# A decode block on one core: w2 taken up in six pieces instead of five, and the first wq issued from ScalarE's queue

## The chip, the core and the metric

The kernel runs on one core of a Trainium2 chip. The metric is the device time of one execution in microseconds, the median of several runs. The profile is of one execution; its span goes from the first instruction to the last, and its times count from the span's start. Engines: PE is TensorE (PEld its weight loads), DVE is VectorE, ACT is ScalarE, POOL is GpSimd, SP is SyncE, which here issues nearly all DMAs. A DMA started by SP stands in SP's queue (SPq), one started by ACT in ACT's (ACTq).

## The reference

One token for each of 4 batch rows goes through an adaptive-layernorm transformer block in float32: attention with 32 query heads on 8 key/value heads over the last 2048 positions of a cache, then a SwiGLU of width 1792, each with a gate. The six modulation vectors come from c:

```
mod = (silu(c) @ w_mod).reshape(4, 6, 1, 512)
sa, ca, ga, sb, cb, gb = mod[:, 0], ..., mod[:, 5]
h = layernorm(x) * (1 + ca) + sa
x = x + ga * attention(h, k_cache, v_cache, wq, wo)   # wq: 512 x 4096, wo: 4096 x 512
h = layernorm(x) * (1 + cb) + sb
x = x + gb * ((silu(h @ w1) * (h @ w3)) @ w2)          # w1, w3: 512 x 1792, w2: 1792 x 512
```

attention: q = h @ wq in 32 heads of 128; of k_cache and v_cache (4 x 8 x 8192 x 128) only the last 2048 positions are used, each kv head by 4 query heads; scores times 128^-0.5, softmax, times v, then @ wo.

## The kernel before, in words

With 4 tokens there is hardly any reuse: every weight and every used part of the cache is read from HBM once, 101 MB in all. The kernel is one stream of large loads on SP's queue, with all compute placed beside it. Each engine has its own program, and semaphores join them. Two SBUF buffers of 8 MB, KV[0] and KV[1], take in turn the k and v of one kv head each (8 heads, `kv_in[g]`); WP (4 MB) takes wo of two heads and wq of the next two.

**The front.** T0 lies in KV[1] and takes t0_in: c and the two parts of w_mod for ca and sa (2 MB). The upper half of WP takes t1_in: wq of the first two heads (2 MB). SP issues T0, then t1, then KV[0], then waits for `pe` >= 1 (the products bM = silu(c) @ w_mod are done with T0) before it loads KV[1]. ACT issues x (8 KB) as its first instruction. VectorE and ACT compute the statistics of x (helpers `stats` and `rroot`, L152 to L169), then, later in both programs, silu(c) (L182 to L188, tile sc). TensorE forms bM from sc, then VectorE forms h (L195), TensorE transposes it, forms the first head's q (bQ, from WP), turns it, and VectorE lays it out in Z (L206). Only then, and once KV[0] has landed, come the first scores (bS from KV and Z).

**The loop.** TensorE runs a loop over 4 pairs of heads: scores, transposed probabilities, values (bO from KV and pT), and the output projection, which gathers in bA. SP issues each load as soon as the buffer it goes to has been read; `s_done`, `o_done`, `q_done`, `a_done` count what TensorE has finished.

**The tail.** After the last head SP issues, behind one another, the rest of w_mod, w1 and part of w3, the rest of w3 in two pieces, gb's part of w_mod (`dgb`), and w2. w2 has 14 chunks of 128 rows (CHUNKS gives their order); W2_CUTS cuts them into pieces, each with its own semaphore dw[i]. hidT holds the hidden activations, transposed. On TensorE, in program order: the two feed-forward products, bM (gb for 4 tokens, four partial sums), then the first HEAD = 8 chunks into bO, 512 columns each, four partial sums at partitions 0, 32, 64, 96; then bT, which sums gb's parts and lays it out by columns (with the 0/1 matrix `same`); then the other six chunks into bX, in the laid-out form, four products of 128 columns for each chunk. VectorE copies bO to y_sb (L459), and four products with `same` add y_sb to bX. ACT copies gb to gb_sb (L448) and bT to gbJ (L465). At the end VectorE multiplies bX by gbJ (yt, L478), adds x (y, L480), and SP stores 64 KB.

Every product goes through one helper line, L266, and most transposes through L287, so in the profile they are told apart by tiles. All SP loads are at L89.

Of the kernel before, what the change touches and what calls it, by code (L numbers as in the profile page):

```python
# [10 lines left out]
B, D, HQ, G, SK, DH, W, FF = 4, 512, 32, 8, 8192, 128, 2048, 1792  # L11
P = 128
# [2 lines left out]
EPS = 1e-5  # L15
CHUNKS = [(j, c) for c in range(4) for j in range(4) if c < 2 or j < 3]
HEAD = 8
W2_CUTS = [0, 8, 10, 12, 13, 14]
PAIRS = G // 2


# [22 lines left out]
def block_kernel(nc, x_in, t0_in, t1_in, kv_in, w_in, wm_in, f1_in, f2_in, gb_in, w2_in, out):  # L44
    T, v, s, gp, S = nc.tensor, nc.vector, nc.scalar, nc.gpsimd, nc.sync

    def sems(names):
        return [nc.alloc_semaphore(n) for n in names.split()]

    def sb(name, cols, rows=P):  # L50
        return nc.alloc_sbuf_tensor(name, (rows, cols), F32).ap()

    def bank(name):
        return nc.alloc_psum_tensor(name, (P, 512), F32).ap()

    (first,) = sems("first")
    A = Queue(nc, s, "act")
    V = Queue(nc, v, "dve")
    L = Queue(nc, gp, "pool")
    dx, dt0, dt1, dkv, dk, dva, dvb, dwo, dm, df1, df2a, df2b, dgb = sems("dx dt0 dt1 dkv dk dva dvb dwo dm df1 df2a df2b dgb")  # L60
    dw = sems(" ".join(f"dw{i}" for i in range(len(W2_CUTS) - 1)))
    z_ok, q_ok, p_ok, k_ok, va_ok, vb_ok, pt_ok, o_ok, ot_ok = sems("z_ok q_ok p_ok k_ok va_ok vb_ok pt_ok o_ok ot_ok")
    s_done, q_done, qt_done, pp_done, o_done, x_done, a_done, pe, last = sems("s_done q_done qt_done pp_done o_done x_done a_done pe last")
# [3 lines left out]
    WP = sb("WP", 8192)  # L67
    T0 = KV[1][:, : 16 + 4096]
    x_sb = sb("x_sb", 512, B)
    ident, same, eps = sb("ident", P), sb("same", B), sb("eps", 1)  # L70
# [3 lines left out]
    q_sb, p_sb, o_sb, a_sb, y_sb, g_sb, u_sb, gb_sb = [sb(n, 512) for n in "q_sb p_sb o_sb a_sb y_sb g_sb u_sb gb_sb".split()]  # L74
# [7 lines left out]
    x1J, gbJ, yt, y = [sb(n, P) for n in "x1J gbJ yt y".split()]  # L82
    zero = y_sb

    bS, bQ, bT, bP, bO, bX, bA, bM = [bank(n) for n in "bS bQ bT bP bO bX bA bM".split()]


    def load(dst, src, sem):
        S.dma_start(dst, src).then_inc(sem, 16)  # L89

    load(T0, t0_in, dt0)
    s.dma_start(x_sb, x_in).then_inc(dx, 16)
    load(WP[:, 4096:], t1_in, dt1)
    load(KV[0], kv_in[0], dkv)
    S.wait_ge(pe, 1)
    load(KV[1], kv_in[1], dk)
# [26 lines left out]
    load(KV[1][:, 6144:8192], gb_in, dgb)  # L123
    for a, b, sem in zip(W2_CUTS[:-1], W2_CUTS[1:], dw):
        load(KV[1][:, 8192 + a * 512 : 8192 + b * 512], w2_in[:, a * 512 : b * 512], sem)
# [139 lines left out]
    def mm(o, lhsT, rhs, start=True, stop=True):  # L265
        return T.matmul(o, lhsT, rhs, start=start, stop=stop, skip_group_check=True)  # L266
# [46 lines left out]
    for k in range(4):  # L313
        for i in range(2):
            ins = mm(bM[32 * i : 32 * i + B, :], sc[:, k * B : (k + 1) * B], T0[:, 16 + (2 * k + i) * 512 : 16 + (2 * k + i + 1) * 512], k == 0, k == 3)
    ins.then_inc(pe, 1)
    T.wait_ge(V.sem, t_h[1])
    for k in range(4):
        ins = T.transpose(bT[:, k * B : (k + 1) * B], h[:, k * P : (k + 1) * P], ident[:B, :B])
# [51 lines left out]
    for k in range(4):  # L371
        for i in range(3):
            at = (3 * k + i) * 512
            ins = mm(bX[32 * i : 32 * i + B, :], sc[:, k * B : (k + 1) * B], KV[0][:, at : at + 512], k == 0, k == 3)
# [19 lines left out]
    for k in range(4):  # L394
        ins = T.transpose(bT[:, k * B : (k + 1) * B], h[:, k * P : (k + 1) * P], ident[:B, :B])
# [4 lines left out]
    def view(t_):  # L400
        return t_.rearrange("p (c j i) -> p c j i", c=4, j=4)
# [4 lines left out]
    for k in range(4):  # L406
        for j in range(4):
            at = 6144 + k * 2048 + j * 512
            ins = mm(bQ[32 * j : 32 * j + B, :], h2T[:, k * B : (k + 1) * B], KV[0][:, at : at + 512], k == 0, k == 3)
# [3 lines left out]
    for k in range(4):  # L413
# [5 lines left out]
        for j in range(3):  # L419
            at = k * 1536 + j * 512  # L420
            ins = mm(bA[32 * j : 32 * j + B, :], h2T[:, k * B : (k + 1) * B], KV[1][:, at : at + 512], k == 0, k == 3)
# [14 lines left out]
    for c in range(4):  # L436
        ins = T.transpose(bS[:, c * P : c * P + 96], u_sb[:96, c * P : (c + 1) * P], ident[:96, :96])
# [6 lines left out]
    for k in range(4):  # L444
        ins = mm(bM[32 * k : 32 * k + B, :], sc[:, k * B : (k + 1) * B], KV[1][:, 6144 + 512 * k : 6144 + 512 * (k + 1)])
    ins.then_inc(pe, 1)
    A.wait((pe, 10))
    t_gb = A.op(s.copy(gb_sb, bM))  # L448
    T.wait_ge(V.sem, t_hid[1])
    hw = view(hidT)  # L450
    w2 = KV[1][:, 8192 : 8192 + 14 * 512].rearrange("p (n m) -> p n m", n=14)
    T.wait_ge(dw[0], 16)
    for n in range(HEAD):
        j, c = CHUNKS[n]
        i = n % 4
        ins = mm(bO[32 * i : 32 * i + B, :], hw[:, c, j, :], w2[:, n, :], n < 4, n >= HEAD - 4)
    ins.then_inc(pe, 1)
    V.wait((pe, 11))
    t_y = V.op(v.tensor_copy(y_sb, bO))  # L459
    T.wait_ge(A.sem, t_gb[1])  # L460
    for j in range(4):
        ins = mm(bT[32 * j : 32 * j + B, :P], same, gb_sb[:, j * P : (j + 1) * P])
    ins.then_inc(pe, 1)
    A.wait((pe, 12))
    t_gb = A.op(s.copy(gbJ, bT[:, :P]))  # L465
    for i in range(1, len(W2_CUTS) - 1):
        T.wait_ge(dw[i], 16)
        for n in range(W2_CUTS[i], W2_CUTS[i + 1]):
            jj, c = CHUNKS[n]
            for j in range(4):  # L470
                ins = mm(bX[32 * j : 32 * j + B, :P], hw[:, c, jj, :], w2[:, n, j * P : (j + 1) * P], n == HEAD, n == 13)
        if i == 1:
            T.wait_ge(V.sem, t_y[1])
            for j in range(4):
                mm(bX[32 * j : 32 * j + B, :P], same, y_sb[:, j * P : (j + 1) * P], False, False)
# [56 lines left out]
```

## Time and profile before

| | before |
|---|---|
| runs, us | 243.27, 244.55, 245.59; median 244.55 |
| the profiled execution, us | 245.33 in all, its span 244.0 |
| mean granted TensorE clock | 0.81 |
| busy: PE / DVE / ACT | 138.5 (57%) / 38.6 (16%) / 25.2 (10%) us |
| DMA | 101.34 MB, mean 415 GB/s over the span |
| HBM read / written | 101.20 MB / 0.07 MB |

A row of the timeline has start and duration in us, engine, line, operation, output tile, input tiles, and in brackets how long the engine was idle before and what ended that. float32 products are recorded as two instructions each, so x16 stands for 8 products. A row on DMA issues has the destination, the source, the issuing queue, how often, the size in KB of one, and the time from issue to landing. A row of stretches has its limits, its length, the busy time of PE, PEld, DVE, ACT and POOL with the number of instructions, the granted clock of TensorE (1.00 is full), the mean busy share of the DMA engines, and GB/s.

### The profile page before, as it was taken

How to read it: one execution, taken by the hardware profiler on the slowest of the kernel's cores; microseconds unless marked ns; L12 is line 12 of the kernel's file. 1: busy time of each engine (PE TensorE's matmuls, PEld its weight loads, DVE VectorE, ACT ScalarE, POOL GpSimd, SP SyncE). 2: the span in 40 equal slices, each digit the busy share in tenths (PEclk: the TensorE clock that was granted, in tenths of full speed). 3: DMA queues.
4: the chain of work that ended last, by engine and by line, in shares of the span. 5: the costliest groups of instructions: out<-in, count | busy, mean ns of one | idle time of the engine just before them, and what ended most of it. 6: DMA issues, size and time to landing. Idle time of an engine off the chain costs nothing. (4 is left out here: it accounts for less than half of the span.)

```text
span 244.0 us, 2237 instructions
## 1 busy us (share of the span) xinstructions
PE 138.5 (57%) x940; PEld 39.2 (16%) x940; DVE 38.6 (16%) x126; ACT 25.2 (10%) x54; POOL 1.7 (1%) x14
## 2 busy tenths in 40 slices
PE   3451047826771477278615763696057758728756
PEld 0010001301220112012101220121012221202203
DVE  6020002202200022022000320220004022150202
ACT  4010001101010021001100210002002111060100
POOL 2000000000000000000000000000000000000000
PEclk9995557988798589767975996779659988997967
DMA  7998999989898989898989898989899999999980
GB/s 255 430 521 346 505 430 430 451 387 500 381 494 365 505 365 496 355 505 365 494 365 494 365 494 355 505 365 494 379 432 446 418 416 434 445 397 426 434 352 16
DMA packets 3901, 101.34 MB, mean 415 GB/s; under 512 B 436, under 2 KB 564, under 8 KB 1080
## 3 DMA queue, kind: packets, MB, share of 16 engines
q1 hardware_dynamic: 3888, 101.26, 96.9%
q8 instruction: 3, 0.05, 0.1%
q10 hardware_dynamic: 8, 0.01, 0.0%
q14 instruction: 2, 0.02, 0.0%
HBM read 101.20 MB, written 0.07 MB: 415 GB/s over the span
## 5 line engine op out<-in xcount | busy, mean ns | idle before, releaser
L266 PE MATMUL bS<-KV,Z 128*16 128x512 f32 x256 | 44.4, 857 | 53.1 <-PEq L269 53.1
L266 PE MATMUL bO<-KV,pT 128*16 128x512 f32 x256 | 31.0, 626 | 0.5
L266 PEld LDWEIGHTS bS<-KV,Z 128*16 128x16 f32 x256 | 9.5, 126 | 82.3 <-issue 82.3
L222 DVE TENSOR_REDUCE MX<-bS 128x1 f32<-128x512 f32 x8 | 5.5, 692 | 95.9 <-PE bS L266 95.9
L230 ACT ACTIVATE p_sb<-bS,NB 128x512 f32<-128x512 f32 x8 | 5.5, 687 | 116.6 <-DVE NB L228 116.6
L287 PE MATMUL bP<-ident,p_sb 128*128 128x128 f32 x32 | 6.2, 329 | 16.6 <-PEq L269 16.6
L266 PE MATMUL bA<-WP,oT 128*4 128x512 f32 x64 | 11.7, 811 | 3.1 <-PEq L269 3.1
L266 PEld LDWEIGHTS bO<-KV,pT 128*16 128x16 f32 x256 | 8.0, 105 | 23.2 <-issue 23.2
L251 ACT ACTIVATE o_sb<-bO,LB 128x512 f32<-128x512 f32 x8 | 5.5, 687 | 47.3 <-PE bO L266 47.3
L287 PE MATMUL bX<-ident,o_sb 128*128 128x128 f32 x32 | 5.0, 280 | 7.2 <-PEq L269 7.2
L266 PE MATMUL bM<-KV,sc 128*4 128x512 f32 x24 | 6.0, 713 | 4.8 <-DVE sc L188 4.8
L266 PE MATMUL bQ<-WP,hT 128*4 128x512 f32 x64 | 8.3, 592 | 0.6 <-DVE hT L197 0.6
L254 DVE TENSOR_REDUCE oT<-bX 128x16 f32<-128x64 f32 x8 | 1.8, 225 | 41.4 <-PE bX L287 41.4
L287 PEld LDWEIGHTS bP<-ident,p_sb 128*128 128x128 f32 x32 | 4.1, 164 | 24.0 <-issue 24.0
L287 PE MATMUL bT<-ident,q_sb 128*128 128x128 f32 x32 | 5.3, 292 | 3.2 <-PEq L269 3.2
L201 ACT ACTIVATE q_sb<-bQ 128x512 f32<-128x512 f32 x8 | 4.7, 593 | 12.5 <-PE bQ L266 12.5
L287 PEld LDWEIGHTS bX<-ident,o_sb 128*128 128x128 f32 x32 | 3.4, 142 | 14.3 <-issue 14.3
L235 DVE COPY pT<-bP 128x256 f32<-128x256 f32 x8 | 3.4, 425 | 14.2 <-PE bP L287 14.2
L266 PE MATMUL bQ<-KV,h2T 128*4 128x512 f32 x32 | 5.1, 799 | 0.3 <-DVE h2T L398 0.3
L266 PE MATMUL bO<-KV,hidT 128*4 128x512 f32 x16 | 3.6, 1047 | 2.7 <-DMA KV<-w_in 2.7
L287 PEld LDWEIGHTS bT<-ident,q_sb 128*128 128x128 f32 x32 | 3.5, 144 | 7.1 <-issue 6.8
L266 PE MATMUL bX<-KV,sc 128*4 128x512 f32 x24 | 4.1, 592 | 0.0
(100 smaller groups left out, 65.4 us busy)
## 6 DMA issues: line engine op xcount, KB each, us to landing
WP<-w_in SPq DMA_DIRECT2D x3, 4096.0 KB, 21.9
KV<-kv_in SPq DMA_DIRECT2D x1, 4096.0 KB, 24.6
KV<-f_in SPq DMA_DIRECT2D x1, 4096.0 KB, 28.1
KV<-kv_in SPq DMA_DIRECT2D x1, 3072.0 KB, 31.4
KV<-wm_in SPq DMA_DIRECT2D x1, 3072.0 KB, 18.7
KV<-f_in SPq DMA_DIRECT2D x2, 1536.0 KB, 19.1
KV<-t_in SPq DMA_DIRECT2D x1, 2056.0 KB, 7.7
WP<-t_in SPq DMA_DIRECT2D x1, 2048.0 KB, 12.2
```

The source lines that it names most:

```text
L201: A.op(s.mul(q_sb, bQ, DH**-0.5), q_ok)
L222: t = V.op(v.reduce_max(MX[:, 0:1], bS, axis=AX.X))
L230: A.op(s.activation(p_sb, bS, AF.Exp, bias=NB[:, 0:1], accum_out=SM[:, 0:1]), p_ok)
L235: v.tensor_copy(pT.rearrange("p (t b c r) -> p c b t r", t=NT, b=B, c=4), bP.rearrange("p (c b i) -> p c b i", c=4, b=B)[:, :, :, :16].rea ...
L251: A.op(s.mul(o_sb, bO, LB[:, 0:1]), o_ok)
L254: V.op(v.tensor_reduce(oT.rearrange("p (r b) -> p r b", r=R), diag, axis=AX.X, op=ALU.add), ot_ok)
L266: return T.matmul(o, lhsT, rhs, start=start, stop=stop, skip_group_check=True)
L287: ins = T.transpose(dst[:, c * P : (c + 1) * P], src[:, c * P : (c + 1) * P], ident)
```

## The change

Two places change. First, W2_CUTS: the 8-chunk first piece of w2 becomes two pieces of 4 chunks, each with its own semaphore. TensorE waits for the first, forms the first four bO products, then bT, then waits for the second, forms the other four, and goes on with bX as before. The signals of bT and bO swap their places in the count `pe`, and the copies gbJ and y_sb wait accordingly. Second, t1 (the first wq) is no longer issued by SP behind T0, but by ACT, as its first instruction; x follows it in ACT's queue, and KV[0] follows T0 at once in SP's.

```diff
-W2_CUTS = [0, 8, 10, 12, 13, 14]
+W2_CUTS = [0, 4, 8, 10, 12, 13, 14]
...
     load(T0, t0_in, dt0)
+    s.dma_start(WP[:, 4096:], t1_in).then_inc(dt1, 16)
     s.dma_start(x_sb, x_in).then_inc(dx, 16)
-    load(WP[:, 4096:], t1_in, dt1)
     load(KV[0], kv_in[0], dkv)
     S.wait_ge(pe, 1)
     load(KV[1], kv_in[1], dk)
...
-    T.wait_ge(dw[0], 16)
-    for n in range(HEAD):
-        j, c = CHUNKS[n]
-        i = n % 4
-        ins = mm(bO[32 * i : 32 * i + B, :], hw[:, c, j, :], w2[:, n, :], n < 4, n >= HEAD - 4)
-    ins.then_inc(pe, 1)
-    V.wait((pe, 11))
-    t_y = V.op(v.tensor_copy(y_sb, bO))
-    T.wait_ge(A.sem, t_gb[1])
-    for j in range(4):
-        ins = mm(bT[32 * j : 32 * j + B, :P], same, gb_sb[:, j * P : (j + 1) * P])
-    ins.then_inc(pe, 1)
-    A.wait((pe, 12))
-    t_gb = A.op(s.copy(gbJ, bT[:, :P]))
-    for i in range(1, len(W2_CUTS) - 1):
+    for i in range(len(W2_CUTS) - 1):
         T.wait_ge(dw[i], 16)
         for n in range(W2_CUTS[i], W2_CUTS[i + 1]):
             jj, c = CHUNKS[n]
+            if n < HEAD:
+                ins = mm(bO[32 * (n % 4) : 32 * (n % 4) + B, :], hw[:, c, jj, :], w2[:, n, :], n < 4, n >= HEAD - 4)
+                continue
             for j in range(4):
                 ins = mm(bX[32 * j : 32 * j + B, :P], hw[:, c, jj, :], w2[:, n, j * P : (j + 1) * P], n == HEAD, n == 13)
+        if i == 0:
+            T.wait_ge(A.sem, t_gb[1])
+            for j in range(4):
+                ins = mm(bT[32 * j : 32 * j + B, :P], same, gb_sb[:, j * P : (j + 1) * P])
+            ins.then_inc(pe, 1)
+            A.wait((pe, 11))
+            t_gb = A.op(s.copy(gbJ, bT[:, :P]))
         if i == 1:
+            ins.then_inc(pe, 1)
+            V.wait((pe, 12))
+            t_y = V.op(v.tensor_copy(y_sb, bO))
+        if i == 2:
             T.wait_ge(V.sem, t_y[1])
             for j in range(4):
                 mm(bX[32 * j : 32 * j + B, :P], same, y_sb[:, j * P : (j + 1) * P], False, False)
```

On TensorE, at the end of the program, the order changes as follows (- before, + now; KV holds w2, hidT the hidden activations, dw0, dw1, ... are the pieces' semaphores, act and dve those of ScalarE and VectorE):

```order
 L266 MATMUL bM<-KV,sc 4x512 x3
 L266 MATMUL bO<-KV,hidT 4x512 [waits dw0,dve]
-L266 MATMUL bO<-KV,hidT 4x512 x7
+L266 MATMUL bO<-KV,hidT 4x512 x3
 L266 MATMUL bT<-gb_sb,same 4x128 [waits act]
 L266 MATMUL bT<-gb_sb,same 4x128 x3
-L266 MATMUL bX<-KV,hidT 4x128 [waits dw1]
+L266 MATMUL bO<-KV,hidT 4x512 [waits dw1]
+L266 MATMUL bO<-KV,hidT 4x512 x3
+L266 MATMUL bX<-KV,hidT 4x128 [waits dw2]
 L266 MATMUL bX<-KV,hidT 4x128 x7
 L266 MATMUL bX<-y_sb,same 4x128 [waits dve]
```

The second four bO products have moved behind bT and wait for a semaphore of their own.

On ScalarE, at the start of the program (WP<-t_in is the first wq, 2 MB):

```order
-L92 DMA x_sb<-x_in 4x512 [waits barrier_Pool_Activation_PE_DVE_SP_release]
+L92 DMA WP<-t_in 128x4096 [waits barrier_Pool_Activation_PE_DVE_SP_release]
+L93 DMA x_sb<-x_in 4x512
 L171 ACT_TABLE_LOAD
 L154 ACTIVATE sq,st<-x_sb,st 4x512 [waits dve]
```

x now stands second in ScalarE's queue, behind the 2 MB of wq; SyncE's row for the same transfer is gone, and the first kv block follows T0 there.

## The prediction

> **What bounds the kernel now.** I read the page first: its slices, its queues and its chain.
>
> ```profile
> GB/s 255 430 521 346 505 430 430 451 387 500 381 494 365 505 365 496 355 505 365 494 365 494 365 494 355 505 365 494 379 432 446 418 416 434 445 397 426 434 352 16
> q1 hardware_dynamic: 3888, 101.26, 96.9%
> ```
>
> One slice is 6.1 us. The load runs at some 430 GB/s from the second slice to the last but one, and SyncE's queue alone (q1) holds the 16 DMA engines for 96.9% of the span. So the middle of the kernel is a stream of 101 MB at one rate, and a change can win only ahead of the stream, behind it, or by a hole in it. The chain of waits, in order of time, shows what stands behind it (start, us):
>
> ```profile
> 208.07 27.21 DMA KV<-w_in
> ...
> 235.41 3.59 PE bO L266 x16
> 239.01 0.43 PE bT L266 x8
> 239.43 2.32 PE bX L266 x56
> 241.78 0.30 DVE yt L478
> ...
> ```
>
> The chain hangs on the first, 8-chunk piece of w2, which lands at 235.3; after it comes 6.5 us of TensorE work in a row. Then I asked for the landings of the later pieces, by the window of their issue (issue start in the first column, then the time to landing):
>
> ```profile
> 207.58 0.44 SPq L89 DMA_DIRECT2D KV<-gb_in  x1
> ...
> KV<-gb_in SPq DMA_DIRECT2D x1, 1024.0 KB, 22.8
> ...
> 208.54 0.43 SPq L89 DMA_DIRECT2D KV<-w_in  x1
> ...
> KV<-w_in SPq DMA_DIRECT2D x1, 512.0 KB, 28.0
> ...
> L89 SPq DMA_DIRECT2D KV<-w_in x2: 432/432/432, 208.5 to 209.0; - x2
> ...
> DMA to landing us min/median/max: 28.0/28.4/28.8
> ...
> L89 SPq DMA_DIRECT2D KV<-w_in x2: 433/2758/5084, 209.5 to 210.0; - x2
> ...
> DMA to landing us min/median/max: 29.0/29.0/29.1
> ```
>
> So gb lands at 207.58 + 22.8 = 230.4, the 2-chunk pieces at 208.5 + 28.0 = 236.5 and 209.0 + 28.8 = 237.8, the 1-chunk pieces at 238.5 and 239.1. The last weights are there at 239.1, but their products end at 239.43 + 2.32 = 241.75: at the end TensorE is 2.65 us behind the stream. That is what a reordering here can win; the 2.2 us behind it (two VectorE steps, the store) stay.
>
> **The w2 pieces, step by step.** The rows of the end, TensorE (PE), its weight loads (PEld) and what they free:
>
> ```profile
> 231.69 1.04 PE L266 MATMUL bM<-KV,sc 128*4 128x512 f32 x8
> 232.80 0.59 ACT L448 COPY gb_sb<-bM 128x512 f32<-128x512 f32 x1 [3.95 <-PE bM L266]
> ...
> 235.41 3.59 PE L266 MATMUL bO<-KV,hidT 128*4 128x512 f32 x16 [2.68 <-DMA KV<-w_in]
> ...
> 238.78 0.15 PEld L266 LDWEIGHTS bT<-gb_sb,same 128*4 128x4 f32 x4 [0.70 <-issue]
> ...
> 238.99 0.79 PEld L266 LDWEIGHTS bX<-KV,hidT 128*4 128x4 f32 x16
> 239.07 0.69 DVE L459 COPY y_sb<-bO 128x512 f32<-128x512 f32 x1 [7.07 <-PE bO L266]
> ...
> 240.27 1.14 PEld L266 LDWEIGHTS bX<-KV,hidT 128*4 128x4 f32 x32
> 240.48 1.22 PE L266 MATMUL bX<-KV,hidT 128*4 128x128 f32 x32
> ...
> 46.28:49.69 3.41, 2.08 (x20) 0.65 (x12) 0.23 (x1) 0.69 (x1) 0.00 (x0) 1.00 1.06 461
> 49.69:53.10 3.41, 0.00 (x0) 0.00 (x0) 0.00 (x0) 0.00 (x0) 0.00 (x0) 1.00 0.74 317
> ...
> 230.60:234.01 3.41, 1.52 (x12) 0.48 (x12) 0.76 (x2) 0.59 (x1) 0.00 (x0) 1.00 0.94 398
> 234.01:237.42 3.41, 2.01 (x12) 0.45 (x16) 0.00 (x0) 0.00 (x0) 0.00 (x0) 0.50 0.95 364
> ```
>
> The last four rows are stretches (second column length, third PE busy, the third from the end the granted clock). The stretch with 1.52 us of PE work is followed by one at clock 0.50, that with 2.08 us by one at 1.00. The 8-chunk group therefore ran at half clock: its chunks follow each other in (238.78 - 235.41)/8 = 0.42 us, where bM at full clock took 1.04/4 = 0.26 with its end. I take 0.42 a chunk at half clock and 0.21 at full, and the same for each set of four 128-wide products that a tail chunk needs (two such chunks: 0.79).
>
> After the change: gb to the old first piece was 235.3 - 230.4 = 4.9 us for 2 MB, so its first half lands at **232.8**, just as bM ends (232.73). Four chunks at full clock: 233.7. gb_sb is ready at 232.80 + 0.59 = 233.4, so bT (0.43 in the chain, at half clock) is done by 234.1, in what was idle time. This adds some 1.1 us of PE work to the 1.52 of that stretch: 2.6, above the 2.08 that held the clock. The second half is due at 235.3, as the whole was. Its four chunks, at full clock: 235.4 to 236.3. The chunks of dw2 (236.5): 237.0. The y_sb copy, 0.69 beside them: done 237.05; its four products: 237.3. dw3 (237.8): 238.3; dw4 (238.5): 238.8; dw5 (239.1): from 239.2 to 239.4. From the last weight load to the last product's end the rows above show 241.70 - 241.41 = 0.3: **239.7** in place of 241.75, 2.05 us less. Every step now waits for its own landing, and what is late next is the last landing. If the clock falls at 237.4 (1.5 to 1.7 us of work in the stretch ahead, between the two known sides), the last four products take 0.42: 239.9. I take 2.05 and keep 1.8 for the range.
>
> The new wait on dw1 stands ahead of all that TensorE has left, and none of it could run sooner. ScalarE's gbJ copy has nothing queued behind it; VectorE's y_sb copy has only yt. The extra issue costs SyncE 0.43 us at 208, 24 us ahead of any landing: nothing. The smaller rows of the split have no price in this trace: at most the half-chunk spacing above, below 0.1 us, since the 512 KB pieces land 1.3 us apart, the pace of 4.9 us for 2 MB.
>
> By the Trainium skill, "DMA: Bandwidth & Descriptors", section "Anatomy of one DMA", a transfer pays about 2.0 us fixed on top of its bytes; by it, if queued transfers paid it one after another, the sum would be -0.05 instead of -2.05. The rows above disagree for transfers queued back to back: 512 KB pieces 1.3 us apart leave no room for it.
>
> **The front.** The first rows, with the landing of wq (t1) and of the first kv block:
>
> ```profile
> 0.73 0.55 ACTq L92 DMA_DIRECT2D x_sb<-x_in  x1
> 0.74 0.38 SPq L89 DMA_DIRECT2D KV<-t_in  x1
> 1.16 0.42 SPq L89 DMA_DIRECT2D WP<-t_in  x1
> 1.64 13.09 SPq L89 DMA_DIRECT2D KV<-kv_in  x2
> ...
> 2.94 0.61 DVE L175 TENSOR_REDUCE st<-x_sb 4x1 f32<-4x512 f32 x1
> ...
> 5.49 0.16 DVE L179 TENSOR_REDUCE same<-ident 128x4 f32<-128x16 f32 x1
> 8.45 0.21 ACT L182 ACTIVATE e<-KV 128x16 f32<-128x16 f32 x1 [3.32 <-DMA KV<-t_in]
> ...
> 9.43 4.93 PE L266 MATMUL bM<-KV,sc 128*4 128x512 f32 x16 [4.82 <-DVE sc L188]
> ...
> 19.75 0.22 DVE L206 TENSOR_REDUCE Z<-bT 128x16 f32<-128x64 f32 x1 [3.22 <-PE bT L287]
> ...
> 34.12 6.24 PE L266 MATMUL bS<-KV,Z 128*16 128x512 f32 x32 [14.41 <-PEq L269]
> ...
> WP<-t_in SPq DMA_DIRECT2D x1, 2048.0 KB, 12.2
> KV<-kv_in SPq DMA_DIRECT2D x1, 32.2
> ...
> 2.00:4.00 2.00, 1.47 (x2) 0.50 (x2) 1.87 (x5) 0.84 (x2) 0.48 (x6) 1.00 0.66 222
> ```
>
> Today t0 lands at about 8.4 and t1 at 1.16 + 12.2 = 13.4. Side by side, t0, t1 and x (behind t1 on ScalarE's queue) all land near 13.4. Then x's statistics, 2.94 to 5.65 today and over before t0 was there, lie ahead of silu on both engines: 2.8 us with the wait, plus 1.0 from silu to the first product (8.45 to 9.43). bM's first product moves from 9.43 to about 17.2, by 7.8 us. Behind it two things wait. Z moves from 20.0 to 27.8, and the scores of the first block start at 34.12 because kv lands at 1.64 + 32.2 = 33.8: 6.3 us of cover. And SyncE's second kv issue, which waits for bM, moves from 14.4 to 22.2; the queue is fed till 33.8: 11.6 us of cover. So the delay costs nothing; beyond the cover it would cost its excess.
>
> Does the stream start sooner? From 2.0 to 4.0 it runs at 222 GB/s where the page's slices show some 430: about 1.0 us is lost in the ramp. The bounds are -1.0 (all of it regained by two queues) and +0.2 (ScalarE's issue takes 0.55 where SyncE's took 0.42). I take 0, by the row that is nearest: t1's issue was over at 1.58 already, so the engines had a second transfer waiting all the while that they ramped.
>
> The Trainium skill, same page, section "Issuing engines are not separate DMA queues", says that issuing from several engines saves only sequencer time; by it the front wins nothing. No row here shows two large transfers on two queues.
>
> **Sum.** -2.05 and 0: the span goes from 244.0 to 241.95, the profiled execution from 245.33 to 243.3. That execution lies 0.78 above the median of the three runs; from 244.55 the same sum gives **242.5**.
>
> **Rivals.**
> - *The ramp is regained too* (25%): two queues fill the engines sooner, some 0.7 of the 1.0 us; 241.8. For it speaks the slow start, against it that t1 was queued in time.
> - *Half clock to the end* (15%): the grant falls before 235.4, as it did. Then bO ends at 237.1, y_sb at 238.1, its products at 238.6, dw3's at 239.4, dw4's at 239.8, dw5's at 240.3, all 240.6: 1.1 us won, 243.4. Against it: 2.6 us of work in the stretch that decides.
> - *The split wins nothing* (4%): the first half lands no sooner than the whole, or each piece pays anew at the end of the stream; 244.5. The 1.3 us spacing speaks against it.
> - *Slower: ScalarE's queue is starved by SyncE's* (4%): t1 and x land behind kv's 8 MB, at 33.8. From x's arrival to bM's end it is 3.8 + 4.9 = 8.7 us, so SyncE issues the second kv at 42.5, and the engines idle for 8.7 us: 242.5 + 8.7 = 251.2. It decides from the point where x lands after 33.8 - 8.7 = 25.1. Against it: x, on ScalarE's queue, was used at 2.94 though t0 was issued beside it.
>
> **Numbers.** The forecast has 52%, with 242.0 to 243.0 as its own range. Runs of before spread 243.3 to 245.6, so under 1% (2.4 us) can't be told from no change. Faster by over 1% is below 242.1: most of the ramp case (23%) and the quick quarter of the forecast (14%), 0.37. Slower: 0.04. The rest, 0.59, within 1%. The range takes in most of the ramp case and most of the half-clock case: 241.4 to 243.8.
>
> **What would show it.** Right: bO's products in two groups, the first near 232.8 and the second near 235.4; bT between them; the last bX products within 0.6 us of the last landing, itself near 239.1; clock 1.00 after 234. Right in front: e's activation near 16, the first scores still near 34. Wrong: a last landing away from 239.1 by over 0.5 us, which moves the time as much; a gap in the DMA slices between 13 and 45 us; scores that wait for Z.

## The result, and the profile after

The changed kernel takes **243.09 us** (median of 17 runs, 242.84 to 243.32), the kernel before 244.59 (median of 17, 243.27 to 245.80). The ratio is 0.9938, with a 95% interval of 0.9918 to 0.9957: 1.5 us faster, within the 1% that the prediction gave 0.59. The profiled execution of the changed kernel has a span of 241.7 us and 243.09 in all; that of before had 244.0 and 245.33.

The two medians hide a difference in shape. The runs of before lie in three groups: 6 from 243.27 to 243.50, 5 from 244.43 to 244.89, 6 from 245.29 to 245.80. The runs of the changed kernel lie within 0.5 us of each other, beside and below the first of these.

The end of the chain of waits, changed kernel (start, us, what):

```profile
210.14 28.79 DMA KV<-w_in
238.93 0.04 issue
238.97 0.45 PE bX L266 x8
239.42 0.02 issue
239.44 0.30 DVE yt L478
239.74 0.02 issue
239.77 0.29 DVE y L480
```

The chain now hangs on the last piece of w2, not on the first; one set of four products is left behind its landing at 238.9. Before, 6.5 us of TensorE work followed the landing that the chain named. TensorE's timeline, and then the granted clock (the third number from the end) in three stretches:

```profile
231.47 1.04 PE L266 MATMUL bM<-KV,sc 128*4 128x512 f32 x8
232.77 1.04 PE L266 MATMUL bO<-KV,hidT 128*4 128x512 f32 x8 [0.26 <-DMA KV<-w_in]
233.62 0.40 PE L266 MATMUL bT<-gb_sb,same 128*4 128x128 f32 x8
235.16 1.04 PE L266 MATMUL bO<-KV,hidT 128*4 128x512 f32 x8 [1.14 <-DMA KV<-w_in]
236.44 0.62 PE L266 MATMUL bX<-KV,hidT 128*4 128x128 f32 x16 [0.24 <-DMA KV<-w_in]
237.02 0.40 PE L266 MATMUL bX<-y_sb,same 128*4 128x128 f32 x8
237.71 1.05 PE L266 MATMUL bX<-KV,hidT 128*4 128x128 f32 x24 [0.29 <-DMA KV<-w_in]
238.97 0.40 PE L266 MATMUL bX<-KV,hidT 128*4 128x128 f32 x8 [0.21 <-DMA KV<-w_in]
```

```profile
230.00:233.00 3.00, 1.94 (x19) 0.61 (x20) 0.89 (x2) 0.42 (x1) 0.00 (x0) 1.00 0.98 408
233.00:235.20 2.20, 1.06 (x20) 0.25 (x16) 0.00 (x0) 0.43 (x2) 0.00 (x0) 1.00 1.02 412
235.20:237.00 1.80, 1.56 (x24) 0.40 (x24) 0.69 (x1) 0.00 (x0) 0.00 (x0) 1.00 1.02 381
```

Each group of products with a piece of w2 waits for its own DMA, by the brackets (the row of x24 holds two pieces); bT and the products of y_sb do not. The clock is 1.00 throughout, where the profile of before had 0.50 from 234.0 to 240.8.

The front, changed kernel: the timeline, the time to landing of wq and of the first kv block, and the rate from 2 to 4 us (last number).

```profile
0.73 0.41 ACTq L92 DMA_DIRECT2D WP<-t_in  x1
1.16 26.33 SPq L89 DMA_DIRECT2D KV<-kv_in  x2
...
17.84 0.67 DVE L175 TENSOR_REDUCE st<-x_sb 4x1 f32<-4x512 f32 x1 [14.81 <-DMA x_sb<-x_in]
...
21.24 5.88 PE L266 MATMUL bM<-KV,sc 128*4 128x512 f32 x16 [16.64 <-DVE sc L188]
...
33.51 0.23 DVE L206 TENSOR_REDUCE Z<-bT 128x16 f32<-128x64 f32 x1 [4.22 <-PE bT L287]
...
33.88 2.56 PE L266 MATMUL bS<-KV,Z 128*16 128x512 f32 x12 [0.41 <-PEq L269]
...
WP<-t_in ACTq DMA_DIRECT2D x1, 2048.0 KB, 12.4
KV<-kv_in SPq DMA_DIRECT2D x1, 31.2
...
2.00:4.00 2.00, 1.47 (x2) 0.50 (x2) 0.97 (x2) 1.06 (x1) 0.47 (x6) 1.00 0.74 271
```

wq lands at 0.73 + 12.4 = 13.1, but x, behind it in the same queue, is used only at 17.84. Z is ready at 33.7, the first kv block lands at 1.16 + 31.2 = 32.4, and the first scores start at 33.88: they now wait for Z, by 1.5 us. They start no later than before (34.12).

### The profile page after: what moved, and what is told of

Same layout as the page of the kernel before. It is cut to its first block, busy times and chain, and to the rows that moved or that the text cites. A ratio compares the mean times of both kernels' runs of the same rounds, so it can differ in the third digit from the quotient of the medians.

```text
span 241.7 us, 2238 instructions
## 1 busy us (share of the span) xinstructions
PE 137.8 (57%) x940; PEld 38.0 (16%) x940; DVE 38.6 (16%) x126; ACT 25.1 (10%) x54; POOL 1.7 (1%) x14
## 3 DMA queue, kind: packets, MB, share of 16 engines
q1 hardware_dynamic: 3888, 99.17, 95.7%
## 5 line engine op out<-in xcount | busy, mean ns | idle before, releaser
L266 PE MATMUL bS<-KV,Z 128*16 128x512 f32 x256 | 42.7, 828 | 39.2 <-PEq L269 39.2
L266 PE MATMUL bO<-KV,pT 128*16 128x512 f32 x256 | 32.5, 652 | 0.5
L266 PE MATMUL bM<-KV,sc 128*4 128x512 f32 x24 | 6.9, 801 | 16.6 <-DVE sc L188 16.6
L287 PE MATMUL bP<-ident,p_sb 128*128 128x128 f32 x32 | 5.6, 303 | 16.6 <-PEq L269 16.6
L266 PE MATMUL bA<-WP,oT 128*4 128x512 f32 x64 | 11.1, 773 | 4.3 <-PEq L269 4.3
L266 PE MATMUL bQ<-WP,hT 128*4 128x512 f32 x64 | 9.2, 647 | 0.6 <-DVE hT L197 0.6
L266 PEld LDWEIGHTS bM<-KV,sc 128*4 128x4 f32 x24 | 1.0, 104 | 22.4 <-DVE sc L188 18.2
## 6 DMA issues: line engine op xcount, KB each, us to landing
WP<-t_in ACTq DMA_DIRECT2D x1, 2048.0 KB, 12.4
```

The costliest lines, as they stand in the source:

```text
L287: ins = T.transpose(dst[:, c * P : (c + 1) * P], src[:, c * P : (c + 1) * P], ident)
```

## The experiments

The prediction took 2.05 us off the tail; the medians moved by 1.5. Theory (clock): the profiled execution of before was one whose eight-chunk group ran at half clock throughout, and other runs of before had less to lose. Rivals: the front gave part of the gain back, or the front made it. Each experiment is compared with runs of the kernel before that were taken beside it; the medians of these lie between 244.45 and 244.75.

### Only the w2 half

```diff
 # the changed kernel, with the front of before
-    s.dma_start(WP[:, 4096:], t1_in).then_inc(dt1, 16)
     s.dma_start(x_sb, x_in).then_inc(dx, 16)
+    load(WP[:, 4096:], t1_in, dt1)
```

> Only the w2 half of the change: pieces of 4, 4, 2, 2, 1, 1; the front is that of the kernel before. Theory (clock): the runs of before lie in groups at 243.3, 244.6 and 245.5, because its eight-chunk group runs at full or at half clock by the phase of the grant; the new order takes the tail off that, and the front is worth 0.15 (the last landing came that much sooner). Then this is 243.2, and its runs lie within 0.6 of each other. Rival (front costs): the tail wins 2.05 and the late x gives 0.5 back; then this is 242.5. Rival (front wins): the front made all of the gain beyond 1.0; then this is over 243.6.

243.30 us, 243.07 to 243.44 in 12 runs; before 244.45; ratio 0.9960 (0.9938 to 0.9982). Its runs lie within 0.4 us of each other, 0.2 above those of the changed kernel. The w2 half alone takes away the groups and makes most of the gain; both rivals fall. (In the 35 runs of before taken beside it, the quick group is set apart, 243.09 to 243.59 and then 244.13; the upper two nearly touch.)

### Only the front half

```diff
 # the kernel before, with the front of the changed one
+    s.dma_start(WP[:, 4096:], t1_in).then_inc(dt1, 16)
     s.dma_start(x_sb, x_in).then_inc(dx, 16)
-    load(WP[:, 4096:], t1_in, dt1)
```

> Only the front half of the change: the first wq on ScalarE's queue ahead of x; w2 as before. Theory (clock): the median moves by -0.15, not to be told from 0, and the runs spread over 2 us as those of before do. Rival (front costs): 0.5 slower, 245.1. Rival (front wins): 0.5 or more faster. In all cases x lands near 17.8 and the first scores wait for Z near 33.9, as in the changed kernel.

244.46 us, 242.74 to 245.44; before 244.45; ratio 0.9982 (0.9953 to 1.0011). The three groups are there: 4 runs from 242.74 to 243.10, 3 from 244.37 to 244.49, 5 from 244.92 to 245.44. The median can't show 0.2 us in such a spread; the expected 0.15 is neither shown nor refuted here. x was used at 17.54 and the first scores started at 33.86, as expected.

### Keeping the clock, w2 uncut

```diff
 # the kernel before
+    for cols in (512, 512, 256):
+        mm(bQ[:, :cols], ident, g_sb[:, :cols])
     T.wait_ge(V.sem, t_hid[1])
     hw = view(hidT)
```

> The kernel before, with three products into a bank that is free by then (512, 512 and 256 columns, 2.1 us at full clock) between bM and the wait for the first w2 piece; their result is not used. Theory (clock): TensorE stays busy enough for full clock, the eight chunks take 1.7 instead of 3.4 us, the tail ends as in the changed kernel: 243.3, runs within 0.6 of each other. Rival (order): what the change won is the order of the pieces, whatever the clock; then this stays at 244.6 with a spread of 2 us.

243.35 us, 242.96 to 243.63; before 244.45; ratio 0.9954 (0.9933 to 0.9975). No piece was cut, no transfer moved; only TensorE did not rest between bM and the first piece. The added products and the eight chunks in its timeline:

```profile
233.42 2.42 PE L266 MATMUL bQ<-g_sb,ident 128*128 128x512 f32 x6
235.77 1.90 PE L266 MATMUL bO<-KV,hidT 128*4 128x512 f32 x16
```

1.90 us instead of 3.59, although the added products let them start 0.36 later. The order of the pieces isn't what won; the clock is. In the change, the new order is what keeps the clock.

### The kernel before, profiled three more times

No edit.

> The kernel before, looked at again for its granted clock at the end. Theory (clock): its time follows the clock under the eight chunks: near 245.4 with 0.50 under all of them, near 243.3 with 1.00, between the two where the grant changes on the way; the last landing is near 239.1 in each. Rival (stream): the groups come from the stream, and the last landing moves with the time.

> A second look at the kernel before. Theory (clock): 245.4 at 0.50 under the eight chunks, 243.3 at 1.00, the last landing near 239.1 all the same. Rival (stream): the last landing moves with the time.

> A third look at the kernel before. Theory (clock): 245.4 at 0.50 under the eight chunks, 243.3 at 1.00, the last landing near 239.1 all the same. Rival (stream): the last landing moves with the time.

The three profiled executions fell into the three groups: 244.83, 245.29 and 243.17 us in all. For each, bM and the eight chunks in the timeline, the clock in the stretch from 235.2 to 237 (and from 239 to 241 where it had fallen), and the issue and the time to landing of the last piece; first the 245.29:

```profile
231.77 1.04 PE L266 MATMUL bM<-KV,sc 128*4 128x512 f32 x8
235.46 3.60 PE L266 MATMUL bO<-KV,hidT 128*4 128x512 f32 x16 [2.64 <-DMA KV<-w_in]
...
235.20:237.00 1.80, 1.54 (x8) 0.29 (x12) 0.00 (x0) 0.00 (x0) 0.00 (x0) 0.50 1.00 384
...
239.00:241.00 2.00, 2.00 (x52) 1.52 (x44) 0.69 (x1) 0.27 (x1) 0.00 (x0) 0.59 0.00 0
...
L89 SPq DMA_DIRECT2D KV<-w_in x1: 5317/5317/5317, 209.8 to 209.8; - x1
DMA to landing us min/median/max: 29.3/29.3/29.3
```

then the 244.83:

```profile
232.19 1.04 PE L266 MATMUL bM<-KV,sc 128*4 128x512 f32 x8
235.72 3.39 PE L266 MATMUL bO<-KV,hidT 128*4 128x512 f32 x16 [2.50 <-DMA KV<-w_in]
...
235.20:237.00 1.80, 1.28 (x8) 0.29 (x12) 0.00 (x0) 0.00 (x0) 0.00 (x0) 0.55 1.00 384
...
239.00:241.00 2.00, 1.83 (x68) 1.40 (x60) 0.69 (x1) 0.27 (x1) 0.00 (x0) 1.00 0.00 0
...
L89 SPq DMA_DIRECT2D KV<-w_in x1: 4877/4877/4877, 210.5 to 210.5; - x1
DMA to landing us min/median/max: 28.9/28.9/28.9
```

and the 243.17:

```profile
232.88 1.04 PE L266 MATMUL bM<-KV,sc 128*4 128x512 f32 x8
235.42 1.90 PE L266 MATMUL bO<-KV,hidT 128*4 128x512 f32 x16 [1.50 <-DMA KV<-w_in]
...
235.20:237.00 1.80, 1.58 (x16) 0.47 (x20) 0.00 (x0) 0.00 (x0) 0.00 (x0) 1.00 1.04 393
...
L89 SPq DMA_DIRECT2D KV<-w_in x1: 4236/4236/4236, 210.8 to 210.8; - x1
DMA to landing us min/median/max: 28.3/28.3/28.3
```

The last landing is at 239.1, 239.4 and 239.1, so it does not order the times; the clock under the eight chunks does. From the 245.29 to the 243.17 the group is 1.7 us shorter and the time 2.1 us. In the 244.83, the clock fell only just ahead of the group and was back before bX; its time lies between.

In stretches of 0.2 us the clock is at 0.50 from 233.8 to 240.6 in the 245.29 (6.8 us, as in the first profile of before), from 235.4 to 238.8 in the 244.83 (3.4 us), and never after 233 in the 243.17. So the groups go with the length of the half-clock spell at the end: about 6.8, 3.4 and 0 us. The brackets show one more difference. The rest ahead of the eight chunks was 2.64, 2.50 and 1.50 us, because in the quick execution bM started at 232.88 instead of 231.77 and 232.19. There the feed-forward products ahead of it had begun later, at 221.63 instead of 220.72 and 221.30, and an earlier spell at 0.50 had slowed them longer, until 226.2 instead of 223.6 and 225.1. So the quick execution did not keep its clock over the same rest; it had a shorter one. That a filled rest keeps the clock was tested above; what shifts the spells from run to run was not.

### x ahead of wq on ScalarE's queue

```diff
 # the changed kernel
+    s.dma_start(x_sb, x_in).then_inc(dx, 16)
     s.dma_start(WP[:, 4096:], t1_in).then_inc(dt1, 16)
-    s.dma_start(x_sb, x_in).then_inc(dx, 16)
```

> The changed kernel with x ahead of the first wq on ScalarE's queue. Theory: x is used at 3 instead of 17.8, Z is ready near 27 instead of 33.7, the first scores start with the landing of the first kv block near 32.4, and the time stays at 243.1, within 0.2, since the stream is not waiting for any of it. Rival (front costs): 0.4 or more faster than the changed kernel.

243.25 us, 243.08 to 243.54; ratio to before 0.9960 (0.9940 to 0.9980). x, bQ's wait for wq, and the first scores:

```profile
3.02 0.68 DVE L175 TENSOR_REDUCE st<-x_sb 4x1 f32<-4x512 f32 x1
...
23.51 1.89 PE L266 MATMUL bQ<-WP,hT 128*4 128x512 f32 x8 [4.22 <-DMA WP<-t_in]
...
34.11 2.76 PE L266 MATMUL bS<-KV,Z 128*16 128x512 f32 x12 [6.82 <-PEq L269]
```

With x used at 3.0, Z was early and the scores had 6.8 us of idle time ahead; the time did not fall. So no cost of the changed kernel's late x shows. The edit moved two more things, so a cost of some 0.2 us could hide. Not expected: wq, which lands at 13.1 in the changed kernel, landed only at 23.5; the first kv block landed at 33.9 instead of 32.4, so the scores still started at 34.1, and from 2 to 4 us the rate was 214 GB/s.

### x behind the first kv block

```diff
 # the changed kernel
-    s.dma_start(x_sb, x_in).then_inc(dx, 16)
     load(KV[0], kv_in[0], dkv)
+    load(x_sb, x_in, dx)
     S.wait_ge(pe, 1)
```

> The changed kernel with x issued by SyncE behind the first kv block instead of behind wq on ScalarE's queue: what the prediction's slower rival would do. x lands near 32.4. From x's arrival to the end of bM it was 9.3 us in the changed kernel, so the second kv block is issued near 41.8 and the stream stands still for some 9.5 to 10.5 us from 32.4: 252.5 to 253.5. Rival (the later cover absorbs it): under 246.

254.19 us (253.97 and 254.41); ratio 1.0395 (1.0336 to 1.0454). x's first use, the second kv issue, the first scores, and a stretch of the DMA engines between (last two numbers):

```profile
32.21 0.68 DVE L175 TENSOR_REDUCE st<-x_sb 4x1 f32<-4x512 f32 x1 [29.19 <-DMA x_sb<-x_in]
...
40.83 0.35 SPq L89 DMA_DIRECT2D KV<-kv_in  x1
...
46.32 4.96 PE L266 MATMUL bS<-KV,Z 128*16 128x512 f32 x32 [0.41 <-PEq L269]
...
33.00:40.00 7.00, 4.38 (x14) 0.77 (x16) 1.63 (x9) 1.42 (x5) 0.00 (x0) 1.00 0.00 0
```

The engines stand still until the issue at 40.83, 8.6 us after x: the length that the prediction's slower rival had. The kernel lost 11.1 against the changed one, some 2.5 more than the gap between x and the issue, and 0.7 more than the upper end of what I expected. I put that down to running dry and starting again, which wasn't measured by itself; of it the trace shows that from 40.8 to 41.4 the engines still moved nothing. So the front is hidden only while the queue is fed: this is the edge of the cover.

### w2 in 14 pieces

```diff
 # the changed kernel; bT, y_sb and its products stay behind chunks 4, 8 and 10
-W2_CUTS = [0, 4, 8, 10, 12, 13, 14]
+W2_CUTS = list(range(15))
```

> The changed kernel with w2 in 14 pieces of one chunk. Theory: a piece costs only its shorter rows, the last landing moves by less than 0.3 us, time 243.1 to 243.4. Rival (fixed price for each transfer, about 2 us if paid one after another, or some part of it at the end of the stream): each of the 8 more pieces costs 0.1 or more, over 243.9.

243.61 us, 243.44 to 243.67; ratio to before 0.9956 (0.9937 to 0.9975), 0.52 above the changed kernel. The last set of products starts 0.51 later than in the changed kernel:

```profile
239.48 0.40 PE L266 MATMUL bX<-KV,hidT 128*4 128x128 f32 x8 [0.23 <-DMA KV<-w_in]
```

Eight more pieces cost 0.52, 0.065 each: more than the theory had, less than the rival. By the Trainium skill, "DMA: Bandwidth & Descriptors", section "Anatomy of one DMA", a transfer issued by GpSimd has a fixed part of about 2 us. These are issued by SyncE, and the prediction left that difference out. The runs do not show such a part by itself; they show that eight more transfers, queued behind one another, do not pay it in turn.

### New front and kept clock, w2 uncut

```diff
 # the kernel before
+    s.dma_start(WP[:, 4096:], t1_in).then_inc(dt1, 16)
     s.dma_start(x_sb, x_in).then_inc(dx, 16)
-    load(WP[:, 4096:], t1_in, dt1)
...
+    for cols in (512, 512, 256):
+        mm(bQ[:, :cols], ident, g_sb[:, :cols])
```

> The kernel before with the new front and with the three products that keep the clock, w2 uncut: 8, 2, 2, 1, 1. Theory (clock): the cut itself is not needed once the clock holds; the front's 0.15 to 0.3 comes on top of the 243.35 that the three products gave with the old front: 243.1, as the changed kernel. Rival (order): over 243.5.

243.18 us, 242.67 to 243.49; before 244.55; ratio 0.9949 (0.9931 to 0.9967). That is the changed kernel's time without the cut, and 0.17 below the same with the old front. No kernel tried here beats the changed one beyond its spread.

## Why the prediction was right or wrong

**The tail's order and the clock: right.** bO came in two groups, at 232.77 and 235.16 (predicted 232.8 and 235.4), bT between them, the clock stayed at 1.00, and bX ended at 239.42 (predicted 239.7). The stretch that decides, 230.60 to 234.01, held 2.76 us of work (2.6 worked out). The one profile has no half clock there, and no time of the 17 runs, at most 243.32, reaches the half-clock rival's 243.4. The two-sided rule behind it, 1.52 us of work against 2.08, was read from two pairs of stretches; the runs bear out that filling the rest keeps the clock, and put no number on how much is needed.

**The sum for the profiled execution: right within 0.25.** 241.95 predicted for the span, 241.7 measured; 0.15 of it is the last landing, 238.9 in place of 239.1.

**The step to the median: wrong in size.** "From 244.55 the same sum gives 242.5" failed: 243.09 lies outside the forecast's own 242.0 to 243.0. It lies inside the stated range only because that range also took in the half-clock rival, which is not what happened; that much was luck. The step took the distance of the profiled execution from the median, 0.78, for a constant of that execution. It was the clock. The profiled execution was one of the half-clock group, where the tail has 2.1 us to lose; of the three later ones, the 243.17 has hardly any. Over the runs of before the tail's gain is 1.15 (244.45 to 243.30, the w2 half alone) where I had 2.05. The signs were in the prediction itself: its half-clock reading of the eight chunks, and three runs that spread over 2.3 us. Priced at full clock, the old tail would have ended near the new one, and the median lay between.

**The front's price: right in sum, wrong in its working.** "All land near 13.4" failed for x, which was used at 17.84; "Z moves to 27.8" became 33.7, and the 6.3 us of cover became a wait of 1.5 us. The second cover, of 11.6 us, shrank to 32.4 - 27.1 = 5.3. The change costs nothing there because the second issue still came before the queue ran dry, and because the first scores, at 33.88, started no later than the 34.12 of before. x landed 4.4 us later than worked out, so that the front's term stayed near 0 was partly luck. Two products were slower as well: bM took 5.88 instead of 4.93, and bQ 1.89 instead of 1.04. The clock was 0.50 under bQ; the profile's row for bM has 1.00, so bM's pace stays unexplained.

**The ramp: mostly not regained.** 271 GB/s from 2 to 4 us instead of 222, 0.23 us at 430. Three pairs say the same: 0.21 (the w2 half alone against the changed kernel), 0.17 (kept clock, old against new front) and 0.16 (x first, where the rate is 214, against wq first). Each is near its spread, and each pair was taken at different times, so about 0.2 is all that can be said. The section "Issuing engines are not separate DMA queues" of the Trainium skill's page "DMA: Bandwidth & Descriptors" allows no more than the saved issue time, 0.42 us there; the runs do not speak against it.

**The rivals.** The starved queue, brought about by moving x behind the kv block, cost 11.1 where I had 8.7. The split's price is 0.065 a piece, as the mean of eight.

## What to carry to other kernels

A gain worked out from one profiled execution holds for that execution; where a stretch of it ran at half clock, ask what the same stretch takes at full clock, and expect the median to gain what the mixture of both gives. A short rest before the last products can cost more than their order, and cutting a transfer so that some work falls into the rest is one way to hold the clock, idle products another. When a small transfer is put behind a large one, look at what else will share the engines while it waits.

## What the runs showed of the hardware that I had not expected

A small transfer landed late while another queue moved large rows. x is four rows of 2 KB; behind wq, which landed at 13.1, it was used at 17.84. With x first, wq needed until 23.5. In both cases the other queue was by then at the kv block, whose rows are 64 KB each. If the queues take turns row by row, each turn of the other costs 64 KB at a sixteenth of 430 GB/s, an estimate of 2.4 us, and two turns fit the 4.7 us. The packet counts fit as well: the profile of before has 3888 packets on SyncE's queue for 27 transfers of 128 rows, 144 for each, and 8 for x's four rows, so a row is not cut into many. The Trainium skill, "DMA: Bandwidth & Descriptors", section "Queues, rings and completion order", says that an engine goes round its queues packet by packet; the times agree, but the size of the rows was not varied, so the cause is argued, not shown.

The granted clock of TensorE at one place of the program differs from run to run: in four profiles of one kernel, the stretch with the eight chunks had 0.50, 0.55, 0.50 and 1.00. Its spells at 0.50 near the end of these profiles lasted about 3.4 or 6.8 us. The mean clock of the whole span says nothing of it: 0.809 in the 243.17, 0.832 in the 244.83 and 0.811 in the 245.29.
